# Keeping the split parts of a weight's Strassen sums in DRAM between two batches, and moving token work to other positions

## The chip, the cores and the metric

One core of a Trainium2 chip runs the kernel. The metric is the device time of one execution in microseconds (us). Before the change three runs took 1289.91 to 1290.56 us, median 1290.46 us.

## The reference

Three stages follow one another, in float32:

```python
# 1. decayed linear attention: 2 batches, 8 heads, 768 tokens, 64 wide
state = gamma * state + k[t] (outer) v[t];   y[t] = scale * q[t] @ state
# 2. mixture of experts: x (1536, 512), 8 experts, every token meets every expert
P = exp(x @ w_gate - max)
for _ in range(8):
    P /= P.sum(1) + 1e-9;  P /= P.sum(0) + 1e-9;  P *= N / E
out = sum over e of  P[:, e] * (relu(x @ w1[e]) @ w2[e])      # w1[e] (512, 1024), w2[e] (1024, 512)
# 3. dense layer: w_in (512, 2048), w_out (2048, 512)
h = x @ w_in
result = (max(h, 0) + alpha * min(h, 0)) @ w_out
```

Nearly all of the arithmetic is in the products with `w1`, `w2`, `w_in` and `w_out`.

## The kernel before

**Split products.** A float32 operand is held as a high part (rounded to the type fp32r, by an ACT copy) and a low part (operand minus high part, by a DVE or POOL subtraction). A product is three matmuls: high by high, high by low, low by high (`mm3`, L239 to L242).

**Seven products for eight.** Each 2x2 block product is formed in Strassen-Winograd's manner with seven smaller products. The blocks of a weight tile are A11, A12, A22, A21; the products also want the sums W1 = A21+A22, W2 = W1-A11, W3 = A21-A11 and W4 = A12-W2 (`w1_sum`). A11, A12, A22 and the four sums are then split. The tokens' side has its own sums, and the seven products are put together by DVE's post-additions (D, E, B, b in the trace).

**Phases.** `PHASES` has 20 entries. 0 to 7 are batch 0 with the eight experts, 8 to 15 (`AGAIN`) batch 1 with the same eight experts, 16 and 17 are the two halves of the dense layer for batch 0's tokens, 18 and 19 the same for batch 1. Phases 8 to 19 (`FAST`) use the seven products in both layers. Such a phase has 56 positions: 28 products of layer 1 and 28 units of layer 2 (two of the units stand ahead of the last product), each of six matmuls. In phases 0 to 7 layer 2 is a plain accumulation.

**W1's tiles.** Tile n = 4 * phase + j (128x1024) is one of the phase's four pieces of W1. In phases 0 to 7 it is loaded (512 KB, `w_load`), POOL forms the four sums in place of A21 and behind it (`w1_adds`), and three parts are split, each by one ACT and one DVE or POOL instruction: a (A11, A12, 512 columns), c (W1, W2, W3, 768 columns), b (A22, W4, 512 columns). Phases 0 to 7 also write the four float32 sums, 1024 columns or 512 KB, to a DRAM tile `c1[n]` (L119). Phases 8 to 15 load A11, A12, A22 (384 KB) and those sums (512 KB), so they do no additions, but they split a, c and b again (`w1_high` on ACT, `w1_low` at L137 on DVE). W2's split sums are treated otherwise: phases 0 to 7 store high and low parts to `c2`, and later phases load them.

**Order of the work.** PE's order is `sequence(ph)`. Everything else is hung on a position of it: `step(ph, pos, fn)` calls `fn` behind that product, and each engine runs its instructions in the order of those calls. So a position fixes what stands ahead of what on DVE, ACT, POOL and SP. All DMAs are issued by SP in one order; eight semaphores take turns, so that a DMA also waits for the landing of the one eight places ahead of it.

**Other work on DVE and POOL** that the change moves past or moves:

- decoding of packed weights (`decode_steps`): `rd` is loaded, L784, L786, L789, L802, L805 on DVE work on 128x512;
- POOL's additions for the dense weights (L219) and `gather` (L1027, POOL, 128x384: the layer's token sums added into `total`), two at each of the positions 2, 5, 8, 11;
- in the dense phases, the additions of layer 2's operands (`t1`, `t2`, `t3`, L942 to L961) and their split (`hhigh`, and `hlow` at L977), all on DVE but for `hhigh`, which is ACT's;
- `x_keep`: split sums of the tokens of batch 1, formed in phases 16 and 17 by ACT and POOL (L301, L309) and stored in DRAM for phases 18 and 19; `x_fetch` loads them.

Of the kernel before, what the change touches and what calls it, by code (L numbers as in the profile page):

```python
# [8 lines left out]
F32 = mybir.dt.float32  # L9
# [37 lines left out]
def tile_kernel(ctx, tc, lead, qkT, kv, ctab, w_gate, w1, w2, w_in, w_out, alpha, out):  # L47
# [8 lines left out]
    pools = {"raw1": stg}  # L56
    tmp = ctx.enter_context(tc.tile_pool(name="tmp", bufs=1))
# [18 lines left out]
    raw = {}  # L76
    ws1, ws2 = {}, {}

    def w_load(kind, n):
# [6 lines left out]
        width = (1792, 1024)[kind]  # L86
        t = (stg, pools["raw1"])[kind].tile([128, width], F32, tag=f"raw{kind}", name=f"raw{kind}_{n}")
        src = (w1, w2)[kind][NJ * e + j] if e < E else wd[kind][NJ * (e - E) + j]
        if ph in AGAIN:
            nc.sync.dma_start(out=t[:, 0:768], in_=src[:, 0:768])  # L90
            nc.sync.dma_start(out=t[:, 768:1792], in_=c1[NJ * e + j])
        else:
            nc.sync.dma_start(out=t[:, 0:1024], in_=src)
        raw[kind, n] = t
# [254 lines left out]
    with tc.manual_schedule():  # L349
# [752 lines left out]
        def at(ph, key, *fns):  # L1102
            hooks.setdefault((ph, key), []).extend(fns)
# [52 lines left out]
        for ph in range(len(PHASES)):  # L1156
# [3 lines left out]
            if ph == 0:  # L1160
                step(ph, 0, lambda: w1_high(1, "c"))
                step(ph, 2, lambda: w1_low(1, "c", dve))
                step(ph, 3, lambda: w1_high(1, "b"))
                step(ph, 4, lambda: w1_low(1, "b", dve))
            elif ph < E:
                decode_at(ph, 30, 31, 32, 33)
                decode_at(ph, 36, 37, 38, 39)
                prep_at(ph, dve, 9, 19, 9, 21, 23, 24, 27)
                prep_at(ph, pool, 25, 25, 25, 29, 30, 30, 31)
                if ph < 7:  # L1170
                    prep_at(ph, dve, 31, 31, 31, 33, 34, 34, 35)
# [35 lines left out]
            if fast:  # L1207
# [46 lines left out]
            if ph + 1 in XGROUP:  # L1254
                g = XGROUP[ph + 1]
                if g > 1:
                    for i, pos in enumerate((20, 21, 22, 23, 25, 26, 28, 30, 34, 36, 42, 43, 45, 46)):
# [40 lines left out]
        def do(ph, key):  # L1298
# [98 lines left out]
```

## Time and profile before

| | before |
|---|---|
| median of three runs | 1290.46 us |
| the profiled execution | 1290.35 us |
| its span in the trace | 1288.5 us |
| PE busy in the span | 98%, 7358 matmuls |
| DVE busy | 82%, 1576 instructions |
| ACT busy | 51%, 1185 instructions |
| POOL busy | 35%, 416 instructions |

Engines in the trace: PE does matmuls, PEld loads weights beside them, DVE, ACT and POOL do elementwise work, SP issues DMAs (SPq is its queue). In a row of instructions, `out<-in` names the tiles, then partitions x elements. A wait row reads: engine, the tile and line that waited, `<-` what it waited for. A row of a window gives, for each engine, the time that it was busy and how many instructions began in it.

The phases start at 45.8, 112.5, 174.9, 236.9, 298.9, 360.8, 422.8, 485.5 (batch 0), 549.4, 609.2, 668.4, 728.5, 793.2, 853.2, 913.2, 978.6 (batch 1), 1040.0, 1102.6, 1166.6 and 1225.8 us (dense).

### The profile page before, as it was taken

What the parts mean: (1) busy time and instruction counts of PE and PEld (TensorE: products, weight loads), DVE (VectorE), ACT (ScalarE), POOL (GpSimd) and SP (SyncE); (2) the same over time, 40 slices, a digit from 0 to 9 for tenths busy, and PEclk for the clock granted to TensorE, in tenths of its full rate; (3) what the DMA queues carried; (4) which work ended last, traced back from release to release, by engine and by line L of the source; (5) the groups of instructions that cost most, each with busy time, mean ns of one, the idle gap of its engine ahead of it and who ended that gap; (6) DMA issues with size and microseconds to landing.
All of it is one profiled execution on the core that took longest, in us unless ns stands there. A gap on an engine that the chain in (4) does not pass through costs nothing.

```text
span 1288.5 us, 20294 instructions
## 1 busy us (share of the span) xinstructions
PE 1262.9 (98%) x7358; PEld 1193.1 (93%) x7358; DVE 1061.0 (82%) x1576; ACT 661.3 (51%) x1185; POOL 448.6 (35%) x416
## 2 busy tenths in 40 slices
PE   9999999999999999999999989999999999999998
PEld 7889898989898989899999989999999999989998
DVE  6677888888897988868889888989798979697866
ACT  5634544435353526464656554646464646564553
POOL 5734261607070707001123422252404365443110
PEclk9999999999999999999999999999999999999999
DMA  9663998998989898699796969688877886597615
GB/s 360 241 229 119 291 316 295 315 301 303 314 299 315 284 325 301 227 320 299 258 346 224 330 216 323 224 291 264 300 231 267 309 272 203 201 311 265 198 65 180
DMA packets 185684, 345.63 MB, mean 268 GB/s; under 512 B 13760, under 2 KB 97264, under 8 KB 185584
## 3 DMA queue, kind: packets, MB, share of 16 engines
q1 hardware_dynamic: 185584, 344.33, 78.8%
q8 instruction: 58, 0.95, 0.3%
q14 instruction: 42, 0.34, 0.1%
HBM read 226.82 MB, written 115.89 MB: 266 GB/s over the span
## 4 chain that ended last, share of the span: by engine, by line
PE 81%; DVE 9%; issue 4%; DMA 3%; ACT 2%; POOL 1%; SPq 0%; DVEq 0%; POOLq 0%; ACTq 0%
PE B L240 9%; PE B L241 9%; PE B L242 9%; PE o L240 6%; PE o L242 6%; PE o L241 6%; PE A L241 6%; PE A L242 5%; PE A L240 5%; PE D L240 3%; PE D L242 3%; PE D L241 3%; PE E L242 3%; PE E L240 3%; PE E L241 3%
## 5 line engine op out<-in xcount | busy, mean ns | idle before, releaser
L969 ACT ACTIVATE hs<-b 128x768 fp32r<-128x768 f32 x168 | 139.7, 841 | 87.8 <-DVE b L942 46.4
L108 POOL TENSOR_TENSOR raw<-raw 128x256 f32<-128x256 f32 x136 | 127.7, 949 | 107.0 <-DMA raw<-wd 64.9
L977 DVE TENSOR_TENSOR hs<-b,hs 128x768 fp32r<-128x768 f32 x144 | 141.6, 990 | 15.1 <-ACT hs L969 14.6
L176 POOL TENSOR_TENSOR pr<-pr 128x256 f32<-128x256 f32 x52 | 49.5, 952 | 204.2 <-DMA pr<-in_w_dram 201.1
L1027 POOL TENSOR_TENSOR total<-total,t 128x384 f32<-128x384 f32 x56 | 80.1, 1454 | 102.2 <-DVE t L1007 102.1
L241 PE MATMUL B<-hs,ws 128*128 128x384 f32 x288 | 96.4, 335 | 1.0 <-DVE hs L977 1.0
L240 PE MATMUL B<-hs,ws 128*128 128x384 f32 x288 | 96.3, 334 | 0.1
L242 PE MATMUL B<-hs,ws 128*128 128x384 f32 x288 | 96.3, 334 | 0.0
L880 ACT ACTIVATE B<-A 128x384 f32<-128x384 f32 x80 | 38.2, 478 | 108.0 <-PE A L242 104.6
L883 DVE TENSOR_TENSOR E<-B,d 128x384 f32<-128x384 f32 x80 | 44.9, 561 | 54.3 <-PE B L242 48.4
L219 POOL TENSOR_TENSOR dr<-dr 128x256 f32<-128x256 f32 x32 | 29.3, 917 | 157.1 <-DVE dw L209 70.4
L309 POOL TENSOR_TENSOR xs<-b,xs 128x384 fp32r<-128x384 f32 x21 | 27.9, 1331 | 153.2 <-ACT xs L305 153.2
L241 PE MATMUL A<-hs,ws 128*128 128x384 f32 x192 | 65.8, 342 | 6.4 <-DVE hs L977 6.4
L242 PE MATMUL A<-hs,ws 128*128 128x384 f32 x192 | 65.0, 339 | 0.0
L240 PE MATMUL A<-hs,ws 128*128 128x384 f32 x192 | 64.9, 338 | 0.0
L180 ACT ACTIVATE pw<-pr 128x1024 fp32r<-128x1024 f32 x32 | 33.8, 1057 | 52.7 <-POOL pr L176 30.0
L794 ACT ACTIVATE ex<-ex,ebias 128x512 uint32<-128x512 uint32 x32 | 23.1, 723 | 64.2 <-DVE ex L784 64.2
L241 PEld LDWEIGHTS B<-hs,ws 128*128 128x128 f32 x288 | 54.0, 188 | 1.5 <-DVE hs L977 1.3
L240 PEld LDWEIGHTS B<-hs,ws 128*128 128x128 f32 x288 | 54.0, 188 | 0.5 <-ACT wa73h L128 0.4
L242 PEld LDWEIGHTS B<-hs,ws 128*128 128x128 f32 x288 | 54.1, 188 | 0.0
L184 DVE TENSOR_TENSOR pr<-pr,pw 128x512 fp32r<-128x512 f32 x64 | 53.4, 866 | 0.0
L176 DVE TENSOR_TENSOR pr<-pr 128x256 f32<-128x256 f32 x76 | 47.8, 629 | 1.7
(3324 smaller groups left out, 4423.8 us busy)
## 6 DMA issues: line engine op xcount, KB each, us to landing
ws<-c SPq DMA_DIRECT2D x168, 512.0 KB, 5.9
raw<-in_w_dram SPq DMA_DIRECT2D x64, 512.0 KB, 4.4
c<-raw SPq DMA_DIRECT2D x32, 512.0 KB, 6.1
pr<-in_w_dram SPq DMA_DIRECT2D x32, 512.0 KB, 5.5
c<-pw SPq DMA_DIRECT2D x32, 512.0 KB, 7.0
c<-pr SPq DMA_DIRECT2D x32, 512.0 KB, 7.1
raw<-c SPq DMA_DIRECT2D x32, 512.0 KB, 6.2
raw<-in_w_dram SPq DMA_DIRECT2D x32, 384.0 KB, 5.3
```

The lines of the kernel that those rows point to most:

```text
L108: eng.tensor_tensor(out=out, in0=in0, in1=in1, op=op)
L176: eng.tensor_tensor(out=out, in0=in0, in1=in1, op=op)
L180: nc.scalar.activation(out=ph2[i], in_=pr[i], func=AF.Copy)
L184: nc.vector.tensor_tensor(out=pr[i][:, a].bitcast(F32R), in0=pr[i][:, a], in1=ph2[i][:, a].bitcast(F32), op=ALU.subtract)
L240: nc.tensor.matmul(ps, ah, bh, start=first, stop=False, skip_group_check=True)
L241: nc.tensor.matmul(ps, ah, bl, start=False, stop=False, skip_group_check=True)
L242: nc.tensor.matmul(ps, alo, bh, start=False, stop=last, skip_group_check=True)
L880: nc.scalar.activation(out=banks[n, "B"], in_=banks[n, "A"], func=AF.Copy)
L883: nc.vector.tensor_tensor(out=banks[n, "E"], in0=banks[n, "B"], in1=banks[n, "d"], op=add)
L969: nc.scalar.activation(out=t[:, 0, :], in_=hsource(ph, k), func=func)
L977: nc.vector.tensor_tensor(out=lo, in0=src, in1=hi.bitcast(F32), op=ALU.subtract)
L1027: nc.gpsimd.tensor_tensor(out=dst, in0=dst, in1=tt[m, h], op=ALU.add)
```

## The change

W's high and low parts become one block of SBUF, 7168 columns wide, with two layouts (`spot`): in phases 0 to 7 and 16 to 19 parts a, b, c in two places each, as before; in phases 8 to 15 a and A22 in two places and W4, W1, W2, W3 in three, one of which lies in other tiles.

Phases 0 to 7 store the high and the low part of the four sums to `c1`: per tile W1, W2, W3 as 2 x 384 KB and W4 as 2 x 128 KB, in runs of 1 KB, instead of one float32 block of 512 KB in runs of 4 KB. The stores stand two positions behind the low part that they wait for (`unkept`). Phases 8 to 15 load A11, A12, A22 as before and the four sums' parts as 4 x 256 KB instead of 512 KB; they leave out part c (one ACT and one DVE instruction of 768 columns per tile) and half of part b (256 of 512 columns). That is 32 ACT and 32 DVE instructions less. SP issues 1022 DMAs instead of 820.

Beside this, work is put at other positions:

- gathers of phases 10 to 15: one at each of 2, 5, 8, 11, 14, 17, 20, 24; those at the end of phase 15, before all eight at its end on POOL, now at 45 to 53 on POOL and the last two on DVE;
- in all `FAST` phases POOL's additions for tiles n+4 and n+5 from positions 18 and 28 to 24 and 34 (phases 8 to 15 have none to do but phase 15, for the dense weights);
- in the dense phases `t2` from 21 to 24, `t3` from 25 and 31 to 33 and 35, two of the splits from 19/20 and 22/24 to 21/23 and 29/30;
- `x_keep`'s 14 pieces from 8 to 93 (positions over 55 mean the next phase) to 29 to 100;
- the last `x_fetch` loads from 34 to 46 to 38 to 51.

```diff
-    wp = ctx.enter_context(tc.tile_pool(name="wp", bufs=2))
+    wp = ctx.enter_context(tc.tile_pool(name="wp", bufs=1))
-    c1 = [drp.tile([128, 1024], F32, name=f"c1_{n}") for n in range(NJ * E)]
+    c1 = [drp.tile([128, 4, 2, 256], F32, name=f"c1_{n}") for n in range(NJ * E)]
...
+    W = wp.tile([128, 7168], F32R, name="W")
+    def spot(n, part, width):
+        s, t = n % 2, (n - NJ * E) % 3
+        at = {"a": 1024 * s, "b": 2048 + 1024 * s, "c": 4096 + 1536 * s}
+        if part in at:
+            return W[:, at[part]:at[part] + width]
+        q = (W4, W1, W2, W3).index(part)
...
+        o = 3584 + 1536 * t + 512 * q if q else 2560 + 1024 * t
+        return W[:, o:o + width]
...
     def w1_high(n, part):
-        if n >= NJ * len(PHASES):
+        kept = n // NJ in AGAIN
+        if n >= NJ * len(PHASES) or kept and part == "c":
             return
-        if part == ("c" if n == 1 else "ac"[n % NJ // 2]) and n < NJ * E:
-            nc.sync.dma_start(out=c1[n], in_=raw[0, n][:, 768:1792])
...
     def w1_low(n, part, eng):
...
+        if n < NJ * E and part != "a":
+            unkept.append([2, n, part, hi, lo])
+    def w1_keep(n, part, hi, lo):
+        for w, t in enumerate((hi, lo)):
+            t = t.bitcast(F32)
+            if part == "b":
+                nc.sync.dma_start(out=c1[n][:, 0, w, :], in_=t[:, 256:512])
+            else:
+                nc.sync.dma_start(out=c1[n][:, 1:4, w, :], in_=t.rearrange("p (a b) -> p a b", a=3))
+    def w1_kept(n, *pieces):
...
+        for piece in pieces or (W1, W2, W3, W4):
+            both = spot(n, piece, 512)
+            src = c1[n - NJ * E][:, (W4, W1, W2, W3).index(piece)]
...
+                nc.sync.dma_start(out=both.bitcast(F32), in_=src.rearrange("p a b -> p (a b)"))
...
+            if ph in AGAIN:
+                step(ph, 0, lambda m=n + 2: w1_kept(m))
+                for pos, piece in ((2, W1), (4, W2), (5, W3), (10, W4)):
+                    step(ph, pos, lambda m=n + 3, piece=piece: w1_kept(m, piece))
+                step(ph, 20, lambda m=n + 4: w1_kept(m))
+                step(ph, 26, lambda m=n + 5: w1_kept(m))
...
-                w1_at(ph, n + 4, pool, dve, 18, 36, 38, 39, 40, 42, 43)
-                w1_at(ph, n + 5, pool, dve, 28, 44, 45, 48, 49, 50, 52)
+                w1_at(ph, n + 4, pool, dve, 24, 36, 38, 39, 40, 42, 43)
+                w1_at(ph, n + 5, pool, dve, 34, 44, 45, 48, 49, 50, 52)
...
-                        step(ph, (2, 5, 8, 11)[q // 2], lambda m=q // 2, h=q % 2: gather(m, h))
+                        step(ph, (2, 5, 8, 11, 14, 17, 20, 24)[q], lambda m=q // 2, h=q % 2: gather(m, h))
...
+                dense = ph >= 2 * E
+                p2, p3, q3 = (24, 33, 35) if dense else (21, 25, 31)
...
-                    for i, key in enumerate((8, 12, 20, 25, 31, 37, 43, 49, 66, 70, 78, 85, 89, 93)):
+                    for i, key in enumerate((29, 33, 38, 42, 46, 50, 66, 73, 80, 86, 90, 94, 97, 100)):
```

Three places of the order in which the engines get their instructions follow. First SP's DMAs near the end of phase 3, before: `c_16<-raw_16` is the store of tile 16's sums, `c_3` and `c_2` are stores of W2's and of the dense weights' parts, `pr`, `raw` and `rd` are loads.

```order
L191 DMA c_2_114<-pr_2908 128x4x256
L119 DMA c_16_96<-raw_16_3075 128x1024
L156 DMA c_3_115<-v14h 128x2x256
L157 DMA c_3_115<-v14h 128x256
...
L93 DMA raw_18_3421<-in_w_dram 128x1024
L810 DMA wd_2_135<-a_2_0_3366 128x512
L774 DMA rd_2_1_3437<-in_w_out_dram 128x1024
L119 DMA c_17_97<-raw_17_3167 128x1024
```

The same place after:

```order
L114 DMA raw_18_3367<-in_w_dram 128x1024
L858 DMA wd_2_135<-a_2_0_3316 128x512
L822 DMA rd_2_1_3383<-in_w_out_dram 128x1024
L214 DMA pr_3407<-in_w_dram 128x1024
L173 DMA c_16_96<-W 128x3x256 x2
L171 DMA c_16_96<-W 128x256 x2
L239 DMA c_3_115<-pw_3385 128x4x256
L239 DMA c_3_115<-pr_3235 128x4x256
```

The store of tile 16's sums was one DMA that stood 14 DMAs ahead of the decode's load `rd`; it is now four DMAs behind that load.

Second, DVE early in phase 11, before: `w..l` are low parts of W1's tile 46, `ex` and `a` belong to the decode, E and `b` are post-additions of layer 1.

```order
L892 TENSOR_TENSOR b_11_8077<-B_8030,d_8041 128x384
L137 TENSOR_TENSOR wa46l<-raw_46_7888,wa46h 128x512
L784 TENSOR_SCALAR ex_2_0_8083<-rd_2_0_7691 128x512
L786 TENSOR_SCALAR a_2_0_8085<-rd_2_0_7691 128x512
L789 SCALAR_TENSOR_TENSOR a_2_0_8085<-rd_2_0_7691,a_2_0_8085 128x512
L137 TENSOR_TENSOR wc46l<-raw_46_7888,wc46h 128x768
L802 SCALAR_TENSOR_TENSOR a_2_0_8085<-a_2_0_8085,ex_2_0_8083 128x512
L805 SCALAR_TENSOR_TENSOR a_2_0_8085<-rd_2_0_7691,a_2_0_8085 128x512
L883 TENSOR_TENSOR E_8126<-B_8095,d_8107 128x384
L137 TENSOR_TENSOR wb46l<-raw_46_7888,wb46h 128x512
```

After:

```order
L159 TENSOR_TENSOR W<-raws,W 128x512
L832 TENSOR_SCALAR ex_2_0_7908<-rd_2_0_7531 128x512
L834 TENSOR_SCALAR a_2_0_7910<-rd_2_0_7531 128x512
L837 SCALAR_TENSOR_TENSOR a_2_0_7910<-rd_2_0_7531,a_2_0_7910 128x512
L850 SCALAR_TENSOR_TENSOR a_2_0_7910<-a_2_0_7910,ex_2_0_7908 128x512
L853 SCALAR_TENSOR_TENSOR a_2_0_7910<-rd_2_0_7531,a_2_0_7910 128x512
L931 TENSOR_TENSOR E_7950<-B_7920,d_7932 128x384
L159 TENSOR_TENSOR W<-raws,W 128x256
```

Ahead of E the subtraction of 768 columns is gone; behind it the one of 512 columns is one of 256.

Third, POOL from the end of phase 15 into phase 16, before: `total` is written by gathers, `raw_66` to `raw_69` by the additions for dense tiles, `xs` by `x_keep`.

```order
L1027 TENSOR_TENSOR total<-total,t_30_11160 128x384
L1027 TENSOR_TENSOR total<-total,t_31_11087 128x384
L108 TENSOR_TENSOR raw_66_11046<-raw_66_11046 128x256 x4
L108 TENSOR_TENSOR raw_67_11138<-raw_67_11138 128x256 x4
L309 TENSOR_TENSOR xs_0_0_11310<-b_3_0_11212,xs_0_0_11310 128x384
L309 TENSOR_TENSOR xs_1_0_11363<-ba_1_11231,xs_1_0_11363 128x384
L108 TENSOR_TENSOR raw_68_11305<-raw_68_11305 128x256 x4
L301 TENSOR_TENSOR b_3_0_11212<-b_3_0_11212 128x384
```

After:

```order
L1075 TENSOR_TENSOR total<-total,t_01_10833 128x384
L1075 TENSOR_TENSOR total<-total,t_11_10846 128x384
L129 TENSOR_TENSOR raw_66_10763<-raw_66_10763 128x256 x4
L129 TENSOR_TENSOR raw_67_10856<-raw_67_10856 128x256 x4
L129 TENSOR_TENSOR raw_68_11013<-raw_68_11013 128x256 x4
L357 TENSOR_TENSOR xs_0_0_11247<-b_3_0_10924,xs_0_0_11247 128x384
L129 TENSOR_TENSOR raw_69_11094<-raw_69_11094 128x256 x4
L357 TENSOR_TENSOR xs_1_0_11299<-ba_1_10941,xs_1_0_11299 128x384
```

`x_keep` starts only behind the additions for tile 68, so its instructions stand later in the phase.

## Rows read from the trace of the kernel before

**Rows 1.** Waits of PE, whole span; after the colon: us in total, times, longest.

```profile
PE B L240 <- DVE E L883: 6.8, 4, 2.9
PE A L241 <- DVE hs L977: 6.4, 5, 1.9
PE B L240 <- DVE b L892: 4.7, 7, 0.9
PE B L241 <- DVE hs L977: 1.0, 1, 1.0
```

**Rows 2.** Windows: start:end length; PE, PEld, DVE, ACT, POOL busy; PEclk, DMA share, GB/s.

```profile
236.90:298.90 62.00, 62.00 (x313) 56.17 (x313) 52.80 (x85) 28.01 (x48) 24.82 (x23) 1.00 0.91 305
609.20:668.40 59.20, 58.73 (x338) 58.29 (x337) 49.83 (x67) 34.13 (x58) 12.90 (x11) 1.00 0.84 293
728.50:793.20 64.70, 60.44 (x338) 59.80 (x337) 53.60 (x71) 33.53 (x56) 16.64 (x13) 0.97 0.80 269
793.20:853.20 60.00, 59.06 (x338) 58.20 (x337) 54.28 (x67) 33.43 (x57) 21.09 (x17) 1.00 0.80 275
913.20:978.60 65.40, 60.74 (x338) 59.78 (x337) 54.46 (x71) 33.51 (x56) 16.26 (x13) 0.97 0.79 266
978.60:1040.00 61.40, 59.86 (x338) 58.13 (x337) 54.39 (x66) 31.46 (x53) 26.60 (x22) 1.00 0.78 278
1040.00:1102.60 62.60, 60.67 (x338) 59.68 (x337) 51.24 (x63) 37.03 (x67) 36.39 (x35) 0.97 0.74 242
1102.60:1166.60 64.00, 60.30 (x338) 57.98 (x337) 54.26 (x69) 34.48 (x61) 27.89 (x26) 1.00 0.74 257
```

**Rows 3.** Windows of 4 us behind two long stalls of PE.

```profile
743.00:747.00 4.00, 3.68 (x12) 3.68 (x13) 2.76 (x5) 1.58 (x2) 3.02 (x3) 0.57 0.80 180
1074.00:1078.00 4.00, 3.65 (x12) 3.65 (x13) 3.06 (x4) 1.28 (x3) 3.55 (x3) 0.59 0.28 102
```

**Rows 4.** Timeline of DVE ahead of the stalls of phases 10 and 11: start, us, instruction.

```profile
678.13 1.77 DVE L137 TENSOR_TENSOR wc42l<-raw,wc42h 128x768 fp32r<-128x768 f32 x1
682.66 1.50 DVE L137 TENSOR_TENSOR wb42l<-raw,wb42h 128x512 fp32r<-128x512 f32 x1
...
738.21 1.76 DVE L137 TENSOR_TENSOR wc46l<-raw,wc46h 128x768 fp32r<-128x768 f32 x1
739.90 1.49 DVE L802 SCALAR_TENSOR_TENSOR a<-a,ex 128x512 f32<-128x512 f32 x1
741.42 1.37 DVE L805 SCALAR_TENSOR_TENSOR a<-rd,a 128x512 uint32<-128x512 uint32 x1
```

**Rows 5.** Timeline of POOL ahead of phase 11's stall.

```profile
733.95 3.79 POOL L219 TENSOR_TENSOR dr<-dr 128x256 f32<-128x256 f32 x4 [7.10 <-DVE dw L209]
737.70 8.32 POOL L1027 TENSOR_TENSOR total<-total,t 128x384 f32<-128x384 f32 x6
```

**Rows 6.** Single instructions by line, ns min/median/max: two of phase 8, two decodes of phase 3.

```profile
L137 DVE TENSOR_TENSOR wc36l<-raw,wc36h x1: 951/951/951, 595.2 to 595.2; 128x768 fp32r<-128x768 f32 x1
L137 DVE TENSOR_TENSOR wb36l<-raw,wb36h x1: 683/683/683, 599.0 to 599.0; 128x512 fp32r<-128x512 f32 x1
L805 DVE SCALAR_TENSOR_TENSOR a<-rd,a x2: 692/902/1112, 280.8 to 295.9; 128x512 uint32<-128x512 uint32 x2
```

**Rows 7.** Timeline of DVE and POOL in phase 17's second half.

```profile
1147.96 1.78 DVE L977 TENSOR_TENSOR hs<-b,hs 128x768 fp32r<-128x768 f32 x1
1147.21 1.72 POOL L309 TENSOR_TENSOR xs<-b,xs 128x384 fp32r<-128x384 f32 x1 [2.71 <-ACT xs L305]
```

**Rows 8.** Windows of 20 us at the highest DMA rates: columns as in rows 2.

```profile
340.00:360.00 20.00, 20.00 (x90) 16.53 (x90) 17.70 (x32) 4.63 (x6) 3.75 (x4) 1.00 1.00 334
600.00:620.00 20.00, 20.00 (x117) 19.99 (x116) 13.27 (x23) 6.30 (x12) 0.00 (x0) 1.00 1.02 376
```

**Rows 9.** Waits of SP's queue in phase 3.

```profile
SPq L119 <- DVE ex L784: 5.7, 1, 5.7
```

**Rows 10.** The page's DMA issues: times, size of each, us from issue to landing.

```profile
raw<-c SPq DMA_DIRECT2D x32, 512.0 KB, 6.2
```

More of the change, by code (lines that the diff above doesn't have):

```diff
@@ L77, in tile_kernel @@
     ws1, ws2 = {}, {}
+    W = wp.tile([128, 7168], F32R, name="W")
+    shared = {}
+    def spot(n, part, width):
[4 more added lines that the diff above has]
+        q = (W4, W1, W2, W3).index(part)
+        if t == 2:
+            if "x" not in shared:
+                shared["x"] = stg.tile([128, 1792], F32R, tag="raw0", name="pairs")
+                shared["y"] = pools["fast"].tile([128, 256], F32R, tag="pair", name="pair")
+            if q == 0:
+                return shared["x"][:, 1536:1792], shared["y"]
+            return shared["x"][:, 512 * q - 512:512 * q]
+        o = 3584 + 1536 * t + 512 * q if q else 2560 + 1024 * t
+        return W[:, o:o + width]
     def w_load(kind, n):
@@ L85, in w_load @@
             return
-        width = (1792, 1024)[kind]
-        t = (stg, pools["raw1"])[kind].tile([128, width], F32, tag=f"raw{kind}", name=f"raw{kind}_{n}")
-        src = (w1, w2)[kind][NJ * e + j] if e < E else wd[kind][NJ * (e - E) + j]
[L89 to L93, printed above, removed]
+        if kind:
+            t = pools["raw1"].tile([128, 1024], F32, tag="raw1", name=f"raw1_{n}")
+        elif ph not in AGAIN:
+            t = stg.tile([128, 1792], F32, tag="raw0", name=f"raw0_{n}")
+        else:
+            if "raw" not in shared:
+                shared["raw"] = stg.tile([128, 1792], F32, tag="raw0", name="raws")
+            t = shared["raw"][:, 768 * (n % 2):768 * (n % 2) + 768]
+        src = (w1, w2)[kind][NJ * e + j] if e < E else wd[kind][NJ * (e - E) + j]
+        width = 768 if ph in AGAIN else 1024
+        nc.sync.dma_start(out=t[:, 0:width], in_=src[:, 0:width])
         raw[kind, n] = t
@@ L115, in w1_high @@
     def w1_high(n, part):
-        if n >= NJ * len(PHASES):
+        kept = n // NJ in AGAIN
+        if n >= NJ * len(PHASES) or kept and part == "c":
             return
-        if part == ("c" if n == 1 else "ac"[n % NJ // 2]) and n < NJ * E:
-            nc.sync.dma_start(out=c1[n], in_=raw[0, n][:, 768:1792])
         if part == "a":
-            ws1[n] = {}
             src, width, pieces = raw[0, n][:, 0:512], 512, (A11, A12)
         elif part == "b":
-            src, width, pieces = raw[0, n][:, 512:1024], 512, (A22, W4)
+            width, pieces = (256, (A22,)) if kept else (512, (A22, W4))
+            src = raw[0, n][:, 512:512 + width]
         else:
             src, width, pieces = raw[0, n][:, 1024:1792], 768, (W1, W2, W3)
-        hi, lo = (wp.tile([128, width], F32R, tag=f"w{part}{w}", name=f"w{part}{n}{w}") for w in "hl")
+        both = spot(n, part, 2 * width)
+        hi, lo = both[:, 0:width], both[:, width:2 * width]
         nc.scalar.activation(out=hi, in_=src, func=AF.Copy)
-        ws1[n][part] = (lo, src, hi)
+        known = ws1.setdefault(n, {})
+        known[part] = (lo, src, hi)
         for q, piece in enumerate(pieces):
-            ws1[n][piece] = (hi[:, 256 * q:256 * q + 256], lo[:, 256 * q:256 * q + 256])
+            known[piece] = (hi[:, 256 * q:256 * q + 256], lo[:, 256 * q:256 * q + 256])
     def w1_low(n, part, eng):
-        if n >= NJ * len(PHASES):
+        if n >= NJ * len(PHASES) or n // NJ in AGAIN and part == "c":
             return
@@ L137, in w1_low @@
         eng.tensor_tensor(out=lo, in0=src, in1=hi.bitcast(F32), op=ALU.subtract)
-        if part == "b":
+        if part == "b" and n != 2 * NJ * E - 2:
             w_load(0, n + 2)
+        if n < NJ * E and part != "a":
+            unkept.append([2, n, part, hi, lo])
+    unkept = []
+    def w1_keep(n, part, hi, lo):
[3 more added lines that the diff above has]
+                nc.sync.dma_start(out=c1[n][:, 0, w, :], in_=t[:, 256:512])
+            else:
+                nc.sync.dma_start(out=c1[n][:, 1:4, w, :], in_=t.rearrange("p (a b) -> p a b", a=3))
+    def w1_kept(n, *pieces):
+        if n // NJ not in AGAIN:
+            return
+        for piece in pieces or (W1, W2, W3, W4):
+            both = spot(n, piece, 512)
+            src = c1[n - NJ * E][:, (W4, W1, W2, W3).index(piece)]
+            if not isinstance(both, tuple):
+                nc.sync.dma_start(out=both.bitcast(F32), in_=src.rearrange("p a b -> p (a b)"))
+                both = both[:, 0:256], both[:, 256:512]
+            else:
+                for w in range(2):
+                    nc.sync.dma_start(out=both[w].bitcast(F32), in_=src[:, w, :])
+            ws1.setdefault(n, {})[piece] = both
     def w2_high(n):
@@ L1256, in tile_kernel @@
                 if g > 1:
[L1257 removed]
+                    for i, pos in enumerate((20, 21, 22, 23, 25, 26, 28, 30, 38, 40, 45, 46, 50, 51)):
                         q = (B11, T1, T2, B21, T3, T4, B22)[i // 2]
@@ L1284, in tile_kernel @@
         at(1, (3, 5), spread_turn)
-        for a in range(KD):
-            at(2 * E - 1, 27, lambda a=a: (gather(a, 0), gather(a, 1)))
+        for pos, m, h in ((45, 0, 0), (46, 1, 0), (48, 2, 1), (49, 3, 1), (52, 0, 1), (53, 1, 1), (55, 2, 0), (55, 3, 0)):
+            step(2 * E - 1, pos, lambda m=m, h=h, pos=pos: gather(m, h, dve if pos > 53 else pool))
         at(0, (0, 1), lambda: gate_logits(NT // 2 - 1, bank("L"), xg[NT // 2 - 1]))
@@ L1307, in do @@
                 fn()
+            for item in list(unkept):
+                item[0] -= 1
+                if item[0] < 0:
+                    unkept.remove(item)
+                    w1_keep(*item[1:])
         for ph in range(len(PHASES)):
```

19 lines of the change are left out of this document (13 added, 6 removed).

## The prediction, made before the result was known

> **What bounds the kernel now.** I read the busy times first, then PE's waits, then the span cut at the starts of the phases, and last the timelines of DVE and POOL ahead of the longest stalls. The reader is to see that PE does matmuls nearly all the time, and that what it waits for is DVE: post-additions E and b of layer 1 (6.8 and 4.7 us) and the splits hs of layer 2's operand (6.4 and 1.0 us) [rows 1]. Where these waits lie is seen in the windows [rows 2]. A phase of seven products without a stall takes 59.2 us; I take that as the floor, since the matmuls are the same in number before and after. Phases 10, 12 and 13 take about 60.0 (one stands in the rows), phase 11 64.7, phase 14 65.4, phase 15 61.4, phase 16 62.6, phase 17 64.0. Over the floor that is 3 x 0.8 + 5.5 + 6.2 + 2.2 = 16.3 us in batch 1, and 3.4 + 4.8 = 8.2 us in the dense layer's first half. In batch 0 (62.0 us, PE busy throughout) there is nothing of the kind; there DMA is near its limit, with a share of 0.91 and 305 GB/s [rows 2].
>
> A long stall costs more than its length: in the 4 us behind phase 11's stall the granted clock is 0.57, behind phase 16's 0.59 [rows 3], the lower of the two levels (1.2 of 2.4 GHz) for most of that time. 4 us at 0.57 lose 1.7 us. That happens in phases 11, 14 and 16, and goes if the stall goes.
>
> **Why DVE is late in phases 11 and 14.** DVE does the 768-column low part in 1.76 us and two steps of the decode in 1.49 and 1.37 us [rows 4]; where nothing runs beside them they take 0.95 and 0.69 [rows 6]. Beside them POOL ran four additions and then six gathers in one go, 733.95 to 746.0 [rows 5]. So 2.3 us of these three, 0.81 + 0.80 + 0.68 rounded, are stretch.
>
> A rule of the Trainium skill bears on that ("SBUF — State Buffer", section "Who interferes with whom"): a DVE instruction that reads two operands from SBUF contends with a GpSimd instruction that reads SBUF, and whoever does not have the access is blocked in full. The rows agree in who stretches, but 0.81 us on the 0.95 is less than a whole POOL instruction of 1.3 us or so. By the rule each POOL instruction moved beside such DVE work costs its whole length; what that would make of the dense phases is the second rival below.
>
> **The change, part by part.** The sum is made against the profiled execution, 1290.35 us, which is 0.11 under the median; I round both to 1290.4.
>
> *Batch 1's splits.* Per tile DVE no longer does 768 columns (0.95 us) and does 256 fewer of the other part (0.951 - 0.683 = 0.27 us) [rows 6]. Four tiles a phase: 4 x 1.22 = 4.9 us out of DVE's 50 to 54 busy us. ACT loses as many instructions, but PE's waits do not name it, so I count nothing. In phases 10, 12 and 13 the phase is 0.8 us over the floor, and ahead of the late post-addition DVE does both kinds, at 1.77 and 1.50 us in phase 10 [rows 4]; without the first and half of the second 2.5 us are gone from the chain, three times the stall. I leave 0.2 us each. In phases 11 and 14 the chain ahead of E loses 1.76 us at once, and the decode's last two steps meet a gather each instead of six in a row (up to 1.5 us of stretch less): together 3.2 against a longest wait of 2.9 us [rows 1], so the stall goes, and the lost clock with it; I leave 0.3 us each. Phase 15 keeps its last gathers, now mostly under its layer 2 instead of at its end; I leave 1.0 of 2.2. Remaining: 0.6 + 0.6 + 1.0 = 2.2, so the gain is 16.3 - 2.2 = 14.1 us. Bounds: if phases 10, 12, 13 and 15 keep theirs (4.6) and 11 and 14 keep 1.3 each, 9; if everything goes, 16.3. I take the upper part, because the removed work stands ahead of the waited-for instruction itself.
>
> *Loads of batch 1.* A tile loads 4 x 256 KB + 384 KB instead of 512 + 384 KB, so 512 KB more: 4 x 0.524 = 2.1 MB in 60 us, 35 GB/s. That makes 301 to 328 of the 266 to 293 GB/s of now [rows 2], and batch 1 has reached 376 [rows 8]. The parts of tile n+3 are issued at positions 2 to 10 for products from position 19 on, those of n+2 at 0 for 12. A position is 59.2 / 56 = 1.06 us, so the shortest lead is about 9.5 us against a landing time of 6.2 [rows 10]. Cost nothing; were the queue 4 us late, it would show as a new DMA wait (third rival).
>
> *Stores of batch 0.* A tile stores 1 MB instead of 512 KB: 4 x 0.524 = 2.1 MB more in 62 us, or 34 GB/s, so 339 instead of 305. Batch 0's own row at a share of 1.00 is 334 GB/s [rows 8]. The share of 0.91 leaves 0.09 x 62 = 5.6 us, and the addition takes 2.1 MB / 334 GB/s = 6.3 us: the queue is just full. Against that the order helps: the old store held SP for 5.7 us behind a DVE instruction [rows 9], with the decode's load 14 DMAs behind it; the new stores stand behind that load. Ends: 2.6 us gained (phases 6 and 7, by their starts 62.7 and 63.9 us long, come to the 62.0 of phase 3) to 21 us lost (3 us in each of seven phases, a little under half of the added transfer, not hidden). I take 1.2 us lost, near the end at which 6.3 against 5.6 us leaves 0.7 a phase, most of it in prefetches that have microseconds to spare.
>
> For that the Trainium skill ("Perfetto Trace Analysis", section "DMA Optimizations") says that transfers under 2 KB carry a marked overhead each, and the new stores go in runs of 1 KB where the old ones went in 4 KB. That batch 0 moves 334 GB/s at a full share where batch 1 moves 376 agrees with it in direction. It speaks for the first rival.
>
> *Dense phases.* What goes: phase 16's 3.4 us, which are a wait of 1.9 for hs [rows 1] and the clock behind it, and of phase 17's waits (64.0 - 60.3 = 3.7 us [rows 2]) all but the 1.0 us wait for hs that stands in its second half: 2.7. Together 6.1, since t2, t3, two splits and the first `x_keep` pieces leave the first half of the phase, where DVE was late. What comes: in the second half of phase 16 POOL has ten `x_keep` instructions instead of six, in phase 17 eight instead of four, and four additions for tile n+5 besides. Such an instruction beside a split stretched it from 0.95 to 1.78 us [rows 6, 7], 0.8 us. DVE is almost full in that half of phase 17, so I count 3 of them on the path there (2.5 us) and 1.5 in phase 16 (1.3 us). Net gain 6.1 - 3.8 = 2.3, from 6 gained to 4 lost (all eight and four of them stretch DVE, and the old waits go only by half).
>
> *The rest* (one block for W, the later `x_fetch` loads, the dense load at position 18 of phase 15): PE's order is the same and dependencies go by the columns of the block, so nothing waits for a neighbour's part; the latest `x_fetch` piece moves 5 positions (5.3 us). I count 0, and up to 2 us lost if that piece becomes late.
>
> Sum: 1290.4 - 14.1 - 2.3 + 1.2 = 1275.2; I say **1275**. This case's own range, from its smaller unknowns, is 1269 to 1282.
>
> **Rivals.** *Batch 0 becomes bound by its DMAs.* For it: 339 against 334 GB/s, shorter runs. Against it: other rates up to 376 in this trace, and the store's wait that no longer blocks the queue. Price 3 us in each of seven phases: 1290.4 - 14.1 - 1.3 + 21 = 1296, slower than before. It decides from 16 / 7 = 2.3 us a phase on.
>
> *POOL beside DVE takes the dense gain back and more.* For it: the full second half of phase 17, the stretch of 0.8 us and the rule above. Against it: DVE's post-additions there read their second operand from PSUM. With 4 us lost there instead of 2.3 gained, and 9 to 11 us gained in batch 1 because spread gathers meet more of DVE's work: 1284.
>
> *The relief does not reach PE.* The decode waits for its load, or the kept parts land late, so that DVE's or PE's waits change their name and keep their length. For it: the one semaphore in eight binds every DMA to an earlier one, and there are 202 more DMAs. Against it: leads of 9 us and more. Half of the dense stalls and a fifth of batch 1's go, batch 0 pays 3: 1290.4 - 3 - 1.4 + 3 = 1289.
>
> **How the numbers follow.** Forecast 0.57, DMA-bound batch 0 0.15, POOL beside DVE 0.15, no relief 0.13. What a measurement of this kernel can tell from no change is about 0.2%, 2.6 us: 1287.8 to 1293.0. Faster: 0.57 + 0.15 and 0.05 from the light end of the third rival, 0.77. Same: 0.09, most of the third rival. Slower: 0.14. The range of 1267 to 1291 leaves out the heavy part of the first rival, and little below.
>
> **What would show it.** Right: phases 10 to 14 at 59.2 to 59.6 us, no window of batch 1 at a clock under 0.9, no wait of PE for E above 0.6 us; batch 0 at 62.0 to 62.3 us with a DMA share near 1.00; phases 16 and 17 at 60 to 62 us with hs the only wait left, in their second halves. Wrong: batch 0's phases at 64 us or more with PE or DVE waiting for a load; a PE wait for W's parts in batch 1; phase 17 at 65 us or more.

## The result, and the profile after

The changed kernel takes 1297.99 us (median of four runs, 1297.32 to 1299.36) against 1290.51 us of the kernel before in the same rounds: a ratio of 1.0057, 95% interval 1.004 to 1.0075. It is slower, where 1275 us was forecast. The profiled execution took 1297.32 us.

Where the time went is told by the lengths of the phases, each taken from its first product to that of the next, phase 19 to the end of DVE's last instruction (us; the last rows are two of the experiments below):

| | 0 to 6 | 7 and 8 | 9 to 15 | 16 and 17 | 18 and 19 |
|---|---|---|---|---|---|
| before | 439.7 | 123.7 | 430.8 | 126.6 | 118.6 |
| changed | 439.6 | 126.5 | 426.2 | 136.2 | 118.1 |
| the kept parts alone (e4) | 439.6 | 126.8 | 420.4 | 126.6 | 118.6 |
| kept parts, two mends (e9) | 439.1 | 125.3 | 413.2 | 125.7 | 118.6 |

Phases 0 to 6 cost nothing, the seam between the batches (phases 7 and 8) 2.8 us, phases 9 to 15 gained only 4.6 us, and the first half of the dense layer lost 9.6.

First the waits of PE in the changed kernel (us in total, times, longest), to be compared with [rows 1].

```profile
PE B L288 <- ACT hs L1017: 7.3, 3, 4.1
PE B L288 <- DVE E L931: 6.4, 8, 1.2
PE B L288 <- DVE b L940: 3.3, 2, 2.1
PE A L289 <- DVE hs L1025: 3.1, 4, 1.1
...
PE tr L1136 <- DVE total L979: 1.5, 1, 1.5
```

The longest wait for E fell from 2.9 to 1.2 us, but there are eight instead of four, and a wait stands on top that was not there: for ACT's part of the split hs.

Windows of phases 3, 8, 11, 14, 16 and 17, with the columns of [rows 2]:

```profile
237.40:299.36 61.96, 61.96 (x314) 56.14 (x312) 52.39 (x85) 27.77 (x47) 24.48 (x21) 1.00 1.01 337
548.99:612.23 63.24, 60.59 (x351) 59.58 (x350) 45.04 (x66) 31.24 (x57) 5.33 (x4) 1.00 0.98 346
730.64:792.98 62.34, 59.51 (x337) 58.23 (x337) 50.01 (x67) 29.84 (x52) 15.79 (x13) 1.00 0.90 311
913.10:977.65 64.55, 60.78 (x337) 59.78 (x337) 50.83 (x67) 29.72 (x52) 15.16 (x13) 0.97 0.87 300
1038.42:1103.94 65.52, 60.83 (x337) 58.08 (x337) 53.38 (x65) 35.81 (x64) 28.22 (x26) 1.00 0.65 217
1103.94:1174.60 70.66, 62.79 (x337) 60.23 (x337) 54.63 (x69) 36.19 (x65) 37.79 (x33) 0.95 0.73 248
```

Phase 3 has 337 GB/s, where 339 were worked out, a share of 1.01, and PE busy throughout. In phase 11 DVE is busy 3.6 us less than before [rows 2], and the phase 2.4 us shorter. Phase 14 is only 0.9 us shorter and its mean clock still 0.97: PE's wait of 2.1 us for b lies there, and from 940.8 to 944.1 us the granted clock is 0.50. In phases 16 and 17 together no engine is busy more than 3 us longer than before; PE stands idle for 12.6 us instead of 5.6 [rows 2].

**The dense phases.** ACT in phase 17 (start, us, instruction, idle time before and what ended it):

```profile
1155.53 0.83 ACT L1017 ACTIVATE hs<-b 128x768 fp32r<-128x768 f32 x1
1156.26 0.62 ACT L149 ACTIVATE W<-raw 128x512 fp32r<-128x512 f32 x1
1166.05 0.52 ACT L353 ACTIVATE xs<-bb 128x384 fp32r<-128x384 f32 x1 [9.17 <-DMA xc<-xs]
1166.48 0.83 ACT L1017 ACTIVATE hs<-b 128x768 fp32r<-128x768 f32 x1
```

ACT stands still for 9.17 us at an instruction of `x_keep`, which wants one of the two xs buffers; the store from that buffer has not landed. Behind it on ACT stands a split hs, for which PE waits 4.1 us. Why the store was late is seen on SP in the same stretch:

```profile
1152.71 0.49 SPq L1036 DMA_DIRECT2D ws<-c  x1
1158.06 0.35 SPq L1071 DMA_DIRECT2D out_dram<-y  x1
1158.46 0.43 SPq L1036 DMA_DIRECT2D ws<-c  x1
1159.40 0.35 SPq L1071 DMA_DIRECT2D out_dram<-y  x1
1159.84 0.38 SPq L360 DMA_DIRECT2D xc<-xs  x1
```

The xs buffer was filled by 1155.1, but SP stood until 1158.06 at a store of y, which DVE had not yet written, and issued the xs store at 1159.84; 6.2 us later ACT goes on. The wait of 7.9 us in phase 16 is of the same make: the buffer was filled by 1087.5, SP stood at a load that waited for a low part on DVE until 1093.7, the store was issued at 1094.19, and ACT went on at 1099.46. All such waits of phases 16 and 17 are in one line of ACT's waits; before there was none:

```profile
ACT xs L353 <- DMA xc<-xs: 18.6, 3, 9.2
```

PE's stall ended at 1167.4 us. Around and behind its end the granted clock is near the lower of its two levels, up to 1173 us:

```profile
1165.50:1169.50 4.00, 1.66 (x4) 1.26 (x5) 2.16 (x2) 3.25 (x5) 2.77 (x3) 0.57 0.63 177
1169.50:1173.00 3.50, 3.50 (x13) 3.50 (x12) 2.93 (x5) 0.00 (x0) 3.42 (x3) 0.52 1.04 358
```

### The profile page after: what moved, and what is told of

It reads as the page before. It is cut to its first block, busy times and chain, and to the rows that moved or that the text cites. A ratio compares the mean times of both kernels' runs of the same rounds, so it can differ in the third digit from the quotient of the medians.

```text
span 1295.6 us, 20588 instructions
## 1 busy us (share of the span) xinstructions
PE 1263.1 (97%) x7358; PEld 1192.6 (92%) x7358; DVE 1035.4 (80%) x1546; ACT 632.6 (49%) x1153; POOL 450.8 (35%) x414
## 4 chain that ended last, share of the span: by engine, by line
PE 73%; DVE 12%; DMA 7%; issue 4%; ACT 2%; SPq 1%; POOL 1%; DVEq 0%; ACTq 0%; POOLq 0%
PE B L288 8%; PE B L289 8%; PE B L290 8%; PE o L288 5%; PE o L290 5%; PE o L289 5%; PE A L289 5%; PE A L288 5%; PE A L290 5%; PE D L290 3%; PE E L288 3%; PE E L289 3%; PE E L290 3%; PE D L288 3%; PE D L289 3%
## 5 line engine op out<-in xcount | busy, mean ns | idle before, releaser
L1025 DVE TENSOR_TENSOR hs<-b,hs 128x768 fp32r<-128x768 f32 x144 | 154.4, 1077 | 19.8 <-ACT hs L1017 18.7
L288 PE MATMUL B<-xh,W 128*128 128x384 f32 x440 | 150.0, 341 | 7.5 <-DVE E L931 4.0
L290 PE MATMUL B<-xh,W 128*128 128x384 f32 x440 | 147.8, 336 | 0.0
L289 PE MATMUL B<-xl,W 128*128 128x384 f32 x440 | 147.7, 336 | 0.0
L224 POOL TENSOR_TENSOR pr<-pr 128x256 f32<-128x256 f32 x52 | 51.9, 999 | 190.4 <-DMA pr<-in_w_dram 62.9
L149 ACT ACTIVATE W<-raw 128x512 fp32r<-128x512 f32 (+1 forms) x144 | 98.5, 694 | 19.4 <-DVE raw L129 19.3
L288 PE MATMUL A<-xh,W 128*128 128x384 f32 x320 | 107.6, 336 | 0.0
L290 PE MATMUL A<-xh,W 128*128 128x384 f32 x320 | 107.4, 335 | 0.0
L289 PE MATMUL A<-xl,W 128*128 128x384 f32 x320 | 107.1, 335 | 0.0
L931 DVE TENSOR_TENSOR E<-B,d 128x384 f32<-128x384 f32 x80 | 45.1, 563 | 64.8 <-PE B L290 58.7
L288 PEld LDWEIGHTS B<-xh,W 128*128 128x128 f32 x440 | 82.7, 188 | 12.8 <-DVE E L931 6.8
L159 POOL TENSOR_TENSOR W<-raw,W 128x512 fp32r<-128x512 f32 (+1 forms) x49 | 76.3, 1572 | 38.2 <-ACT W L149 19.2
L159 DVE TENSOR_TENSOR W<-raw,W 128x512 fp32r<-128x512 f32 (+1 forms) x95 | 86.8, 929 | 2.8 <-ACT W L149 2.8
L289 PEld LDWEIGHTS B<-xl,W 128*128 128x128 f32 x440 | 82.8, 188 | 0.3
```

The lines of the kernel that those rows point to most:

```text
L224: eng.tensor_tensor(out=out, in0=in0, in1=in1, op=op)
L288: nc.tensor.matmul(ps, ah, bh, start=first, stop=False, skip_group_check=True)
L289: nc.tensor.matmul(ps, ah, bl, start=False, stop=False, skip_group_check=True)
L290: nc.tensor.matmul(ps, alo, bh, start=False, stop=last, skip_group_check=True)
L931: nc.vector.tensor_tensor(out=banks[n, "E"], in0=banks[n, "B"], in1=banks[n, "d"], op=add)
L1025: nc.vector.tensor_tensor(out=lo, in0=src, in1=hi.bitcast(F32), op=ALU.subtract)
```

## The experiments

All are timed against the kernel before on the same chip; ratios are with 95% intervals. There were three sets of rounds, e1 to e4, e5 to e8, and e9 with e10, in which the kernel before took 1292.18, 1290.45 and 1291.06 us; across sets the ratios are to be compared, not the times. Lengths of phases are from the one profiled execution of each run.

**e1: `x_keep` where it was.**

```diff
-                    for i, key in enumerate((29, 33, 38, 42, 46, 50, 66, 73, 80, 86, 90, 94, 97, 100)):
+                    for i, key in enumerate((8, 12, 20, 25, 31, 37, 43, 49, 66, 70, 78, 85, 89, 93)):
```

> The changed kernel with x_keep's 14 pieces back at positions 8 to 93; all else as changed. Theory A (the pieces, three or four positions apart, wait on ACT for a buffer whose store has not landed, and the splits of layer 2's operand queue behind them): phases 16 and 17 come back from 136.2 us to about 127, so some 1289 us, and no wait of ACT for a store of xs is left in the profile. Theory B (POOL's work beside DVE in the second halves stretches DVE): the same time, since the POOL work leaves the second half too. Theory C (t2, t3 and the two splits, which were moved later, make layer 2's operands late): phases 16 and 17 stay at 134 us or more, 1296 us.

1288.92 us, 0.9977 (0.9968 to 0.9985). Phases 16 and 17 take 126.8 us, 9.4 less than in the changed kernel, and ACT waits for no xs store. Theory C is out: t2, t3 and the two splits are at their new places here and cost nothing that can be seen. A and B are not told apart by this run.

**e2: a third xs buffer.**

```diff
+            third[0] += g == 3
+            if g == 3 and third[0] % 3 == 2:
+                t = held[q] = tp.tile([128, 1024], F32R, tag="rd", bufs=1, ...)[:, 0:2 * HT]...
+            else:
                 t = held[q] = pools["fast"].tile([128, 2, HT], F32R, tag="xs", bufs=2, ...)
```

> The changed kernel, x_keep's pieces where the change put them, with a third buffer for every third piece (the decode's load buffer, free since phase 15). Nothing else differs, and DVE, ACT and POOL do the same work at the same positions. Theory A: most of the loss in phases 16 and 17 goes, 7 us or more, 1291 us or less. Theory B: within 2 us of the changed kernel's 1298.

1296.02 us, 1.0033 (1.0021 to 1.0044). By the total the expectation of A was missed. By the phases it was met where it spoke: 16 and 17 take 128.7 us, 7.5 less, with the same POOL work at the same positions. But phase 18 takes 63.2 us instead of 58.7 (in an execution that was 2.3 us under the median). Waits of ACT in phases 16 to 18 (two lines), of PE from phase 16 on, and of SP in phases 17 and 18; the last line is SP's in phase 17 of the changed kernel:

```profile
ACT n L908 <- DMA out_dram<-y: 4.0, 1, 4.0
ACT xs L359 <- DMA xc<-xs: 1.8, 1, 1.8
```

```profile
PE B L288 <- ACT B L934: 2.7, 1, 2.7
```

```profile
SPq L371 <- DMA xc<-xs: 13.5, 3, 4.9
```

```profile
SPq L365 <- DMA xc<-xs: 12.7, 3, 5.1
```

ACT's wait for xs stores is down from 18.6 to 1.8 us. What is left is SP's: `x_fetch` (L371) loads what those stores have just written, SP waits 13.5 us in all for them to land, the stores of y behind it come late, and in phase 18 ACT wants a y buffer, with B behind it, for which PE waits 2.7 us. SP's wait is not new, it was 12.7 us in the changed kernel; there phase 18 began 8 us later, and ACT had no such wait. So the late `x_keep` has two ways to PE, through ACT's queue and through SP's; the second is read from the trace, and no run takes it away alone. Theory B stands for the rest at most: 128.7 against 126.6 us before.

**e3: gathers in pairs again.**

```diff
-                        step(ph, (2, 5, 8, 11, 14, 17, 20, 24)[q], ...gather(m, h))
+                        step(ph, (2, 5, 8, 11)[q // 2], ...gather(m, h))
```

> The changed kernel with the gathers of phases 10 to 15 back in pairs at positions 2, 5, 8, 11. Theory D (the gathers at 14 to 24 stretch DVE ahead of post-additions in the middle of the phase, and so make the waits of 0.84, 1.22 and 2.08 us): these go and phases 9 to 15 get 4 to 7 us shorter than the changed kernel's 426.2, about 1292 us. Theory E (spreading did not matter, or helped): phases 9 to 15 stay within 1.5 us or get longer.

1292.7 us, 1.0001 (0.9992 to 1.0009). Phases 9 to 15 take 420.4 us, 5.8 less than in the changed kernel: D. Phase 10 shows it. DVE in the changed kernel ahead of a late E:

```profile
693.53 1.39 DVE L837 SCALAR_TENSOR_TENSOR a<-rd,a 128x512 f32<-128x512 uint32 x1
694.84 1.77 DVE L1025 TENSOR_TENSOR hs<-b,hs 128x768 fp32r<-128x768 f32 x1
...
697.52 0.56 DVE L931 TENSOR_TENSOR E<-B,d 128x384 f32<-128x384 f32 x1
```

POOL beside it:

```profile
692.02 2.35 POOL L1075 TENSOR_TENSOR total<-total,t 128x384 f32<-128x384 f32 x2
694.33 1.47 POOL L349 TENSOR_TENSOR b<-b,b 128x384 f32<-128x384 f32 x1
```

And DVE in e3, with the gathers gone from there:

```profile
694.88 0.69 DVE L837 SCALAR_TENSOR_TENSOR a<-rd,a 128x512 f32<-128x512 uint32 x1
695.49 0.95 DVE L1025 TENSOR_TENSOR hs<-b,hs 128x768 fp32r<-128x768 f32 x1
```

That is 0.70 and 0.82 us of stretch in two instructions, the first beside the gathers, the second beside an addition of `x_keep` (L349) that stands behind them on POOL. PE's wait of 0.84 us in that phase is gone in e3, and the phase takes 58.4 us instead of 59.6.

**e4: the kept parts alone.** The edits of e1 and e3, and all other positions as before the change (the additions at 18 and 28, t2, t3, the splits, `x_fetch`, the end of phase 15).

> The changed kernel with every move of positions undone (gathers, the end of phase 15, additions at 18 and 28, t2, t3, splits, x_keep, x_fetch): only the kept high and low parts and the block for W are left. Theories A and D together: phases 16 and 17 at about 127 us, phases 9 to 15 at 420 us or less, batch 0 to phase 8 as in the changed kernel (+2.8 us): 1283 us. If the kept parts relieve nothing by themselves: phases 9 to 15 at 430 us, 1293 us.

1283.0 us, 0.9931 (0.9917 to 0.9944): as expected. Phases 9 to 15 take 420.4 us, 16 and 17 126.6, as before the change, and 7 and 8 126.8. Against the changed kernel that is 5.8 and 9.6 us, what e3 and e1 had given; the moves that no run tests alone cost next to nothing.

**e5: the moves alone**, in the kernel before.

> The kernel before with all the moves of positions and nothing else: no kept parts, no block for W. If moves and kept parts add up: the changed kernel was 15 us above the kept parts alone, so 1290.5 + 15 = 1305 us, with phases 16 and 17 at about 136 us and phases 10, 12 and 13 about 1 us longer than before. If the moves only cost because of the kept parts' layout and loads: 1290 us, phases 16 and 17 at 127.

1307.31 us, 1.0125 (1.0105 to 1.0145). Phases 16 and 17 take 135.2 us, and 10, 12 and 13 61.5 instead of 60.0. The two halves add up: 0.9931 x 1.0125 = 1.0055, against 1.0057 of the changed kernel.

**e6: the seam.** With the kept parts alone, the first kept loads come earlier in phase 7.

```diff
-                step(ph, 30, lambda: w1_kept(NJ * E))
-                step(ph, 33, lambda: w1_kept(NJ * E + 1))
+                step(ph, 24, lambda: w1_kept(NJ * E))
+                step(ph, 29, lambda: w1_kept(NJ * E + 1))
```

> The kept parts alone, with the first two tiles' kept parts loaded in phase 7 at positions 24 and 29 instead of 30 and 33. Theory F (these eight loads, 2 MB, stand ahead of the decode's load and the stores of tt at the end of phase 7, and make DVE late): phases 7 and 8 come from 126.8 us to about 124, 1280 us. Rival G (the queue is full there whatever the order, since phases 7 and 8 have more to load): phases 7 and 8 stay within 1 us of 126.8.

1279.18 us, 0.9923 (0.9907 to 0.994). Phases 7 and 8 take 124.3 us, 2.5 less: F by the phases. By the ratio, 0.9923 against 0.9931 of e4, the gain is 1 us and not clear of the noise. But with the kept loads at 30 and 33 the two phases took 126.5 to 127.5 us in six traces (the changed kernel, e1 to e4, e7), and with the edit 124.3 and 125.3 (e6, e9). What was wrong is seen in the changed kernel. SP at the end of phase 7:

```profile
537.05 0.33 SPq L822 DMA_DIRECT2D rd<-in_w_out_dram  x1
538.41 2.29 SPq L182 DMA_DIRECT2D W<-c  x4
...
549.32 0.33 SPq L114 DMA_DIRECT2D raws<-in_w_dram  x1
```

DVE's waits in phases 7 and 8 (`tt` holds batch 0's turned totals on their way to DRAM):

```profile
DVE ex L832 <- DMA rd<-in_w_out_dram: 5.5, 2, 4.1
...
DVE ex L832 <- DMA xd<-tt: 4.1, 1, 4.1
DVE a L834 <- DMA xd<-tt: 2.8, 1, 2.8
```

In the kernel before, the third is missing and the others are short:

```profile
DVE ex L784 <- DMA rd<-in_w_out_dram: 1.7, 1, 1.7
...
DVE ex L784 <- DMA xd<-tt: 0.7, 1, 0.7
```

Two sets of kept loads of 1 MB (the second at 538.41) stand about a decode's load and a store of tt that DVE needs for its buffers. DVE waits in the middle of its queue, the totals behind it come late, and PE waits 1.5 us for one of them 3 us into batch 1 (`tr` in the first rows above). In e6:

```profile
DVE ta L316 <- DMA c<-pr: 4.5, 1, 4.5
DVE ex L832 <- DMA xd<-tt: 3.1, 1, 3.1
...
DVE ex L832 <- DMA rd<-in_w_out_dram: 2.0, 2, 1.3
```

```profile
PE tr L1136 <- DVE total L979: 0.5, 1, 0.5
```

The three waits are down from 12.4 to 5.1 us, but another, for a store of W2's parts (`c<-pr`), is up from 0.7 to 4.5: a part of the delay only moved.

**e7: later decodes in phases 11 and 14**, with the kept parts alone.

```diff
-                    decode_at(ph, 13, 14, 15, 17)
-                    decode_at(ph, 24, 25, 26, 28)
+                    decode_at(ph, 16, 17, 18, 20)
+                    decode_at(ph, 27, 28, 29, 31)
```

> The kept parts alone, with the second and third decode of phases 11 and 14 three positions later (13 to 17 become 16 to 20, 24 to 28 become 27 to 31). Theory H (DVE's relief in these phases was spent waiting for the decode's load, 2.2 and 1.0 us in phase 11, since the load is issued only behind the step before it and has one buffer): the waits for rd shrink under 0.5 us each and phases 11 and 14 fall from 62.9 and 63.4 us by 1.5 to 3 us each, 1279 us. Rival I (DVE has too much work there in any order): within 1 us of the kept parts alone, 1283 us, with other waits of the same sum.

1277.1 us, 0.99 (0.9886 to 0.9914). Phases 11 and 14 fall from 62.9 and 63.4 us to 59.9 both, 6.4 in all: H, and a little more than was expected. By the ratios e7 is 4 us under e4. DVE in e4 in phase 11, and in the kernel before:

```profile
744.70 1.18 DVE L159 TENSOR_TENSOR W<-raws,W 128x512 fp32r<-128x512 f32 x1
748.11 0.43 DVE L832 TENSOR_SCALAR ex<-rd 128x512 uint32<-128x512 uint32 x1 [2.23 <-DMA rd<-in_w_in_dram]
```

```profile
746.50 0.95 DVE L137 TENSOR_TENSOR wc47l<-raw,wc47h 128x768 fp32r<-128x768 f32 x1
748.45 0.43 DVE L784 TENSOR_SCALAR ex<-rd 128x512 uint32<-128x512 uint32 x1 [1.00 <-DMA rd<-in_w_in_dram]
```

In e4 DVE waits 2.23 us for the decode's load where before the change it did a low part of 0.95 us and then waited 1.0 us. With the decode three positions later no wait of DVE for rd is left in the phase.

**e8: more stores in batch 0**, with the kept parts alone.

```diff
                 nc.sync.dma_start(out=c1[n][:, 0, w, :], in_=t[:, 256:512])
+                nc.sync.dma_start(out=again[n][:, w, :], in_=t[:, 256:512])
```

> The kept parts alone; phases 0 to 7 store W4's high and low parts a second time to DRAM that nobody reads: 2 x 128 KB per tile, 1.05 MB per phase, 3.1 us of the queue's time at 339 GB/s. Batch 0's DMA share was already 1.01 in phases 3 to 5. Theory J (the queue is full, and what is added is not hidden): 2.5 to 3.1 us more in each of six or seven phases, 1300 us or more. Rival K (the share counts time that a fuller queue can still use): batch 0 stays within 3 us in all, 1284 us.

1291.33 us, 1.0012 (1.0002 to 1.0022), 0.8% over e4: between the two theories. In the trace phases 3 to 7 are 1.2 us longer each than in e4 (317.2 against 311.0 us in all) and phase 8 4.3 us; its profiled execution, at 1295.7 us, is 4.4 us over the median of the runs, so these are rather too large. Phase 4 of e8, and the decode's load in it:

```profile
302.80:365.90 63.10, 62.07 (x313) 56.10 (x312) 51.74 (x85) 28.04 (x47) 24.12 (x23) 1.00 1.01 348
```

```profile
DVE ex L834 <- DMA rd<-in_w_out_dram: 2.3, 1, 2.3
```

The share is 1.01 as in the changed kernel, but 348 GB/s move instead of 337. So the share of 1.01 was not yet the limit, and of the 3.1 us added per phase some 1.2 reach PE, by way of the decode's load: DVE waits 1.4 to 4.5 us for it in each of the phases 3 to 7, where in e4 it does so in phase 7 alone (3.4 us).

**e9 and e10: both mends, and the decodes alone.** e9 is e4 with the edits of e6 and e7; e10 is the kernel before with the edit of e7.

> The kept parts alone with both mends: the first kept loads at positions 24 and 29 of phase 7, and the later decodes of phases 11 and 14. If the two are independent: 1283.0 less 2.5 us (phases 7 and 8) less 6.4 us (phases 11 and 14), 1274 us. If DMA traffic moved out of phase 7 or the decodes meet each other's gain: 1277 us or more.

> The kernel before, with only the later decodes of phases 11 and 14. Theory H (the wait for the decode's load took what the kept parts had relieved, and before the change DVE's own work filled most of that time): phases 11 and 14, 64.7 and 65.4 us, fall by 2 us each at the most, since the work ahead of E in the first chain, with its stall of 2.9 us and the lower clock, is untouched; 1287 us. Rival L (the early decodes alone made these phases slow, and the kept parts have little to do with it): both phases fall to 60 to 61 us, 1281 us.

e9: 1273.88 us, 0.9867 (0.9853 to 0.9882), the fastest of all. e10: 1286.27 us, 0.9962 (0.995 to 0.9974), with phases 11 and 14 at 63.1 us both, so 1.7 and 2.3 less than before: H, though the second is over the 2 us that were its most. In these two phases together the kept parts alone gain 3.9 us, the later decodes alone 3.9, and both 10.3.

## Why the prediction was wrong

By the traces the change lost 7.1 us where the sum had 15.2 gained. Of the 22.3 us between, 11.9 are the dense phases, 5.8 the gathers, 3.7 the rest of batch 1 and 1.6 the seam; about 0.6, gained elsewhere, go the other way.

- **The dense phases** were the step that failed most: 2.3 us gained were forecast, 9.6 lost. The first stalls did shrink, as was worked out (the first wait for hs of phase 16 from 1.9 to 0.4 us). For what comes instead, the prediction counted only POOL's stretch of DVE (3.8 us) and named no queue behind the moved instructions. But one of `x_keep`'s four steps is ACT's, with two buffers and a store and its landing in the loop. At the two long waits a buffer's way, from ACT's copy into it to the landing of its store, took 13.6 and 12.6 us, of which 6.7 and 4.8 us were SP standing at other instructions. The piece that takes the same buffer next stands 8 and 6 positions later there (8.5 and 6.3 us), against 11 to 15 for most pieces before. So ACT stands still, and behind it on ACT wait the splits that PE needs. e2 shows that the buffers make most of the loss (7.5 of 9.6 us), e1 that all of it goes with the positions of `x_keep`. The second rival had the place and the sign, but another mechanism and under half of the price (4 us). The prediction's own sign of being wrong, phase 17 at 65 us or more, came with 70.7.
- **The gathers**: "the decode's last two steps meet a gather each instead of six in a row" was counted as relief. In phase 11 it was none: POOL starts late there and runs five gathers in a row all the same. In the other phases the gathers at 14 to 24 met DVE work that had been alone. Together 5.8 us lost (e3), at the price per instruction that the prediction had itself (0.8 us), on instructions that it did not look at.
- **Batch 1's relief** in phases 11 and 14: "the stall goes, and I leave 0.3 us each" failed. The first stall fell from 2.9 to 1.2 us, but DVE's free time there turned into a wait for the decode's load (e4, e7, e10). That was the third rival's mechanism, in two phases of seven. With all moves undone the kept parts gain 10.4 us in phases 9 to 15 (e4), inside the bounds of 9 to 16.3 but not the 14.1. The 17.6 us of e9 are not theirs alone: the later decodes gain 3.9 us without them (e10), and some 3 us come only with the edits together. That e9 ends near the forecast of 1275 us is chance, since it holds two mends that the change lacks. In e9 phases 10, 12 and 13 fall to 58.4 us, under the 59.2 that was taken as the floor; the phase that gave that floor has PE busy for 58.7 us of it [rows 2].
- **Batch 0's stores** were right in rate (337 against 339 GB/s) and in effect: phases 0 to 6 did not change. The 1.2 us were set too low for the seam, where kept loads come on top: 2.8 us. The rival that gave 1296 us, near the 1298 measured, is not what happened, for it put its 21 us in phases 1 to 7.
- **Loads of batch 1**: PE waits for no kept part. Only two loads of W2's parts (ws) are late, by 0.8 us in all. At the seam the kept loads do cost time, by way of DVE (e6).
- **Sums of the rivals**: the third takes 1.4 us as a fifth of batch 1's 14.1, which is 2.8 (1288 instead of 1289); the first has 1.3 us of dense gain where the forecast has 2.3, and the second leaves out the 1.2 us of the stores. None of these decides anything here.

What stays open: how much of the 2.1 us that e2 leaves in phases 16 and 17 is POOL's stretch of DVE, and how much of phase 8's 61.0 us in e9 (59.8 before) is due to the kept loads still there.

## What to carry to other kernels

When an instruction is moved, ask not only what it costs but what it waits for at its new place. With a ring of two buffers, twice the spacing of the instructions has to exceed the whole way of a buffer: being filled, standing in the queue that issues the store, and the landing. Otherwise everything behind the instruction on its in-order engine waits too. A relieved engine runs on to its next wait; if that is a load that stands ahead of the work that the matmuls need, the relief is lost until the two change places. And a change made of two halves is worth timing by halves: here one gains 0.7% and the other loses 1.25%.

## What was not expected of the hardware

A DMA share of 1.01 was measured at 337 GB/s and, with more stores (e8), at 348 GB/s: a share near one is not yet the end of the rate. Stores in runs of 1 KB instead of 4 KB lowered it little, if at all (phase 3 has 337 GB/s; from 340 to 360 us it was 334 at a share of 1.00 before [rows 8] and is 327 at 1.01 after).

The lower clock does not follow from the length of a stall alone. In phase 16 PE waits 1.9 us for the same split hs in the kernel before, e4 and e10 as in e6, e7 and e9. In the first three about 3.4 us at the lower clock follow, in the others none. The stretches right behind that wait, in e4 and in e6:

```profile
1067.50:1070.90 3.40, 3.40 (x12) 3.40 (x12) 2.46 (x3) 1.32 (x3) 2.91 (x3) 0.50 0.32 116
```

```profile
1064.00:1067.40 3.40, 3.40 (x20) 3.40 (x21) 2.45 (x3) 1.11 (x2) 3.14 (x3) 1.00 0.32 105
```

Phase 16 takes 62.6 us in the first three and 61.8 in the others. So 0.8 of the 0.9 us by which phases 16 and 17 are shorter in the last row of the table above (e9) are the clock's and not the mends'. Behind phase 11's stall of 1.2 us in e4 the clock stays at 1.00, while behind the 4.1 us stall of phase 17 it was still 0.52 from 1169.5 to 1173.0 us.
